# Four f32 matmuls whose results nobody reads, in TensorE's waits from the last piece of W_up to chunk 2 of W_down

## Chip, cores, metric

One core of one Trainium2 chip. The metric is the device time of one execution in microseconds (us); the profile's span, from its first to its last instruction, is some 1.3 us shorter. "The granted clock" is the share of its full speed at which TensorE is let run; the profile records it; "warm" and "cold" stand for 1.00 and 0.50. A "landing" is the arrival of a transfer's data. In the profile PE is TensorE, PEld its weight load, DVE VectorE, ACT ScalarE and SPq the queue that issues transfers; PSUM is the memory that TensorE writes.

## The reference, cut to what matters

A decode step: layer norm, attention over the last 4096 positions of a cache (4 sequences, 16 kv heads, 32 query heads), output projection and residual, then layer norm and a gated MLP with residual. The change touches the MLP.

```python
x = A_x                                                        # [4, 1, 576], bf16
h = x + _A_ref(_layernorm(x), A_k_cache, A_v_cache, A_wq, A_wo)
# _B_ref(layernorm(h), W_gate, W_up, W_down):
gate = jnp.einsum("bsd,df->bsf", x, W_gate)                    # F = 4608
up   = jnp.einsum("bsd,df->bsf", x, W_up)
hh   = gate * (gate > 0) * up
out  = h + jnp.einsum("bsf,fd->bsd", hh, W_down)
```

## The kernel before

All large inputs come through one DMA queue in one fixed order: wq, the K and V tiles, wo, W_gate, W_up, W_down. A transfer is only held back until the reader of the room it overwrites is done (in before the issue of W_down stood still 7.3 us for TensorE's line 34). W_down comes as chunks 0, 1 and 2 (1296 KB each) and chunk 3, split into rows 0-2, 3-5, 6-7 and 8 so that little work is left behind the last landing. The end of the kernel:

```python
for g in range(2):                       # 0: gate, 1: up
    for c in (4, 0, 1, 2, 3):            # c == 3 of up is a landing of its own
        part_ = c if c == 4 or (c == 3 and g) else 0
        for m in range(3):
            for j in range(4):
                deps = [("L", "gu", g, part_)] if first else []
                ...                      # 12 matmuls, 384 columns, 4 column groups side by side
# ... ReLU on ACT, product on DVE ("HH") ...
for r in range(9):                       # hh transposed by TensorE
    pe(("HTR", r), lambda e, r=r, dst=dst: e.transpose(...), [("HH", m) ...])
# ... copies to SBUF; two f32 and two bf16 matmuls start the sum with h ...
for j in range(4):                       # chunks of W_down
    for r in range(9):
        for n in range(2):               # 2 matmuls of 288 columns, side by side
            deps = []
            if n == 0:
                if r == 0 or (j == 3 and r in (3, 6, 8)):
                    deps.append(("L", "wd", j, r))       # waits for the landing
                ...
            pe(("DOWN", n), lambda e, ...: e.matmul(bank[n][...], ...), deps)
dve("OUT0", ...)                         # copy out, then the output DMA
```

`pe(name, fn, deps)` appends an instruction to TensorE's stream. TensorE's matmuls run in this order, and one that waits holds up those behind it (dose5 below shows the order: chunk 2 starts at 374.19 us, behind its fillers; late_idle shows the waiting: its 53 matmuls behind the one that names a wait name none, and all start after it, from 374.49 us).

## Time and profile before

| | before |
|---|---|
| time, median of the first three runs | 377.86 us (377.85 to 378.06) |
| span of the profiled execution | 376.6 us |
| TensorE busy | 208.8 us (55%) |
| DMA | 159.59 MB, 98.8% of the span, 424 GB/s |
| landing of rows 6 and 7 of chunk 3 (374.00 us) to last matmul's end | 0.74 us |
| end of the wait for row 8, the last piece (374.39 us), to last matmul's end | 0.35 us |

The page of before has the DMA queues with the share of the 16 engines' span that their packets took, and under its fourth heading the chain that ended last:

```profile
q1 hardware_dynamic: 6776, 159.59, 98.8%
...
DMA 56%; PE 21%; DVE 20%; issue 1%; SPq 1%; ACT 0%
```

The queue is busy nearly all the time. That points to a kernel bound by bytes; skip_chunk1 tests it below. Next the end of its chain of waits, in order of time (start, length, what):

```profile
341.69 32.31 DMA sb_arena<-in_B_W_down_dram
374.00 0.04 issue
374.04 0.70 PE psb L705 x6
374.74 0.43 DVE sb_out_sb L708
```

One copy closes the kernel. The timeline of before, TensorE only (start, length, engine, line, operation; in brackets how long the engine idled before it, and what ended that):

```profile
361.94 0.35 PE L667 MATMUL psb<-sb_arena,sb_hnT 128*32 128x384 bf16 x4 [0.71 <-DMA sb_arena<-in_B_W_up_dram]
...
363.95 0.27 PE L682 MATMUL psb<-sb_ident_b,sb_pp 128*128 128x128 bf16 x1 [1.34 <-DVE sb_pp L676]
...
368.13 1.16 PE L705 MATMUL psb<-sb_arena,sb_pp 128*32 128x288 bf16 x16 [1.37 <-DMA sb_arena<-in_B_W_down_dram]
...
371.23 1.03 PE L705 MATMUL psb<-sb_arena,sb_pp 128*32 128x288 bf16 x14 [1.82 <-DMA sb_arena<-in_B_W_down_dram]
...
373.33 0.55 PE L705 MATMUL psb<-sb_arena,sb_pp 128*32 128x288 bf16 x6 [0.46 <-DMA sb_arena<-in_B_W_down_dram]
374.04 0.66 PE L705 MATMUL psb<-sb_arena,sb_pp 128*32 128x288 bf16 x6 [0.17 <-DMA sb_arena<-in_B_W_down_dram]
...
374.39 0.10 PEld L705 LDWEIGHTS psb<-sb_arena,sb_pp 128*32 128x32 bf16 x2 [0.24 <-DMA sb_arena<-in_B_W_down_dram]
```

The brackets are TensorE's gaps, all but one here ended by a landing. The table of windows of before gives for each stretch the busy time and instruction count of each engine, then the granted clock, the DMA share and GB/s:

```profile
core 0: us, PE busy (x) PEld busy (x) DVE busy (x) ACT busy (x) POOL busy (x), PEclk, DMA share, GB/s
355.00:358.40 3.40, 3.40 (x44) 0.63 (x16) 0.00 (x0) 0.00 (x0) 0.00 (x0) 0.50 0.92 393
...
361.30:363.90 2.60, 0.67 (x12) 0.10 (x4) 1.49 (x3) 0.00 (x0) 0.00 (x0) 1.00 1.00 421
...
369.50:371.20 1.70, 0.00 (x0) 0.00 (x0) 0.00 (x0) 0.00 (x0) 0.00 (x0) 1.00 0.94 385
```

The clock was 0.50 in the first half of the MLP but 1.00 in all windows after 361.3 us, also in the gaps.

### The profile page before, as it was taken

The numbers are of one execution on the slowest core, as the hardware profiler recorded it, in microseconds if no ns is written. First come the engines' busy times: TensorE is split into PE (matmuls) and PEld (weight loads), VectorE is DVE, ScalarE is ACT, GpSimd is POOL, SyncE is SP. The second block draws the span as 40 slices with busy tenths as digits, with TensorE's granted clock in tenths as the row PEclk, the third lists the DMA queues.
The fourth block names the chain that finished last, engine by engine and source line by source line (L and its number), as shares of the span: only waits on it lengthen the run. The fifth ranks groups of instructions, "written<-read, shape, count | busy, mean of one in ns | idle before, by whom it ended". The sixth has DMA issues, their size and how long they took to land.

```text
span 376.6 us, 2562 instructions
## 1 busy us (share of the span) xinstructions
PE 208.8 (55%) x1456; PEld 37.6 (10%) x703; DVE 226.2 (60%) x164; ACT 54.3 (14%) x85; POOL 10.5 (3%) x29
## 2 busy tenths in 40 slices
PE   0304443249919191749282845664655687886674
PEld 0000000001101010001010100100000001002422
DVE  3078888779292959584847777665659423333220
ACT  3193000301000114010101140101010401112010
POOL 8200000000000000000000000000000000000000
PEclk9955888859968797687788796989696968998699
DMA  8999999999999999999999999999999999999996
GB/s 335 446 439 428 416 442 439 428 418 442 437 425 421 439 440 421 421 442 442 425 419 439 442 428 418 438 439 428 425 435 439 423 425 439 422 431 425 437 413 260
DMA packets 6802, 159.74 MB, mean 424 GB/s; under 512 B 764, under 2 KB 904, under 8 KB 1672
## 3 DMA queue, kind: packets, MB, share of 16 engines
q1 hardware_dynamic: 6776, 159.59, 98.8%
q8 instruction: 8, 0.13, 0.1%
q10 hardware_dynamic: 16, 0.01, 0.0%
q14 instruction: 2, 0.02, 0.0%
HBM read 159.58 MB, written 0.00 MB: 424 GB/s over the span
## 4 chain that ended last, share of the span: by engine, by line
DMA 56%; PE 21%; DVE 20%; issue 1%; SPq 1%; ACT 0%
DMA sb_arena<-in_A_k_cache_dram 48%; DVE sb_arena L425 16%; PE psb L34 13%; DMA sb_arena<-in_B_W_down_dram 9%; PE psb L449 4%; PE psb L510 3%; DVE sb_o_tmp L523 1%; DVE sb_pp L488 1%; PE psb L476 1%; SPq L284 0%; DVE sb_pp L471 0%; DVE sb_hx L454 0%; ACT sb_pp L468 0%; PE psb L705 0%; DVE sb_out_sb L708 0%
## 5 line engine op out<-in xcount | busy, mean ns | idle before, releaser
L425 DVE STREAM_TRANSPOSE sb_arena<-sb_arena 128x8192 f32<-128x8192 f32 (+1 forms) x19 | 139.9, 7365 | 66.4 <-DMA sb_arena<-in_A_k_cache_dram 66.4
L449 PE MATMUL psb<-sb_arena 128*32 128x512 bf16 x256 | 44.5, 640 | 118.8 <-DVE sb_arena L425 118.8
L34 PE MATMUL psb<-sb_arena,sb_pp 128*128 128x512 bf16 x382 | 107.3, 389 | 2.9 <-issue 2.8
L510 PE MATMUL psb<-sb_arena,sb_pp 128*128 128x512 bf16 x115 | 44.8, 389 | 8.9 <-DVE sb_o_tmp L523 8.9
L34 PE MATMUL psb<-sb_arena 128*32 128x512 bf16 x256 | 45.4, 645 | 0.0
L520 ACT COPY sb_o_tmp<-psb 32x512 f32<-32x512 f32 x32 | 18.5, 577 | 181.7 <-PE psb L34 181.4
L523 DVE TENSOR_TENSOR sb_o_tmp<-psb,sb_fm 32x512 f32<-32x512 f32 x32 | 21.7, 678 | 18.6 <-PE psb L34 18.1
L449 PEld LDWEIGHTS psb<-sb_arena 128*32 128x32 bf16 x256 | 9.7, 117 | 162.0 <-DVE sb_arena L425 131.8
L510 PEld LDWEIGHTS psb<-sb_arena,sb_pp 128*128 128x128 bf16 x128 | 12.8, 100 | 115.7 <-issue 115.7
L527 DVE TENSOR_REDUCE sb_o_sel<-sb_o_tmp 128x128 f32<-128x512 f32 x16 | 17.7, 1107 | 0.5
L468 ACT ACTIVATE sb_pp<-psb,sb_hx 128x1024 bf16<-128x1024 f32 x4 | 4.5, 1113 | 79.4 <-DVE sb_hx L465 79.4
L488 DVE TENSOR_TENSOR sb_pp<-psb,sb_m 128x1024 bf16<-128x1024 f32 x8 | 9.3, 1206 | 4.6 <-PE psb L476 4.6
L483 ACT ACTIVATE sb_pp<-psb,sb_m 128x512 bf16<-128x512 f32 x16 | 9.8, 698 | 14.6 <-PE psb L476 14.6
L526 DVE TENSOR_TENSOR sb_o_tmp<-sb_o_tmp,sb_fm 64x512 f32<-64x512 f32 x16 | 11.0, 689 | 0.5
L416 ACT COPY sb_arena<-sb_q_keep 32x256 bf16<-32x256 bf16 x8 | 9.7, 1448 | 0.1
L402 DVE CAST sb_pp<-psb 128x512 bf16<-128x512 f32 x1 | 2.4, 2425 | 10.1 <-PE psb L382 10.1
L471 DVE STREAM_TRANSPOSE sb_pp<-sb_pp 128x1024 bf16<-128x1024 bf16 x4 | 5.0, 1245 | 5.1 <-ACT sb_pp L468 5.1
L476 PE MATMUL psb<-sb_pp,sb_to_v 128*32 128x256 bf16 x64 | 4.3, 400 | 6.2 <-DVE sb_pp L471 6.2
L705 PE MATMUL psb<-sb_arena,sb_pp 128*32 128x288 bf16 x72 | 5.4, 288 | 3.8 <-DMA sb_arena<-in_B_W_down_dram 3.8
L708 DVE CAST sb_out_sb<-psb 32x288 bf16<-32x288 f32 x1 | 0.4, 446 | 9.7 <-PE psb L705 9.7
L454 DVE TENSOR_REDUCE sb_hx<-psb 128x1 f32<-128x1024 f32 x4 | 4.9, 1225 | 2.3 <-PE psb L34 2.3
L34 PE MATMUL psb<-sb_arena,sb_hnT 128*32 128x384 bf16 x80 | 6.3, 394 | 0.0
(123 smaller groups left out, 80.4 us busy)
## 6 DMA issues: line engine op xcount, KB each, us to landing
sb_arena<-in_A_k_cache_dram SPq DMA_DIRECT2D x16, 4096.0 KB, 26.1
sb_arena<-in_A_v_cache_dram SPq DMA_DIRECT2D x16, 4096.0 KB, 28.6
sb_arena<-in_A_wo_dram SPq DMA_DIRECT2D x1, 4608.0 KB, 25.3
sb_arena<-in_B_W_gate_dram SPq DMA_DIRECT2D x1, 4608.0 KB, 26.9
sb_arena<-in_A_wq_dram SPq DMA_DIRECT2D x1, 4096.0 KB, 13.1
sb_arena<-in_B_W_down_dram SPq DMA_DIRECT2D x3, 1296.0 KB, 30.9
sb_arena<-in_B_W_up_dram SPq DMA_DIRECT2D x1, 3456.0 KB, 27.8
sb_arena<-in_B_W_up_dram SPq DMA_DIRECT2D x1, 1152.0 KB, 30.3
```

Of the source, the lines that this page charges most:

```text
L34: return e.add_instruction(mybir.InstMatmult(name=e.bass.get_next_instruction_name(), engine=mybir.EngineType.PE, ins=[e.lower_ap(rhs), e. ...
L416: act("QW", lambda e, i=i, q=q: e.copy(out=bass.AP(tensor=arena, offset=32 * i * AW + 2 * i + q, ap=[[AW, 32], [512, 16], [136, 4], [32, 4]]),
L425: dve(("TRA", g), lambda e: e.transpose(out=dst, in_=src), [("L", "K", g)] if lo == 0 else [])
L449: fn = lambda e, out_=out_, lhsT=lhsT, rhs=rhs, start=start, stop=stop: e.matmul(out_, lhsT=lhsT, rhs=rhs, start=start, stop=stop, skip_gr ...
L476: pe(("RM", b, n // 2), lambda e, n=n, i=i: e.matmul(bank[6 if n < 2 else 0][32 * i:32 * i + 32, n % 2 * 256:n % 2 * 256 + 256], lhsT=to_v ...
L483: act(("EV", b, 0), lambda e, a=a: e.activation(out=bass.AP(tensor=pp, offset=2 * a, ap=[[PPW, 128], [8, 2], [32, 128], [1, 2]]), in_=bank ...
L488: dve(("EV", b, 1), lambda e, n=n: e.tensor_tensor(out=bass.AP(tensor=pp, offset=16 + 8 * n, ap=[[PPW, 128], [32, 128], [2, 4], [1, 2]]), ...
L510: fn = lambda e, lhsT=lhsT, rhs=rhs, k=k, j=j: e.matmul(bank[2 + j], lhsT=lhsT, rhs=rhs, start=(k == 0), stop=(k == 7), skip_group_check=True)
L520: act(("OSC", g), lambda e, j=j: e.copy(out=o_tmp[32 * j:32 * j + 32, 0:512], in_=bank[2 + j][32 * j:32 * j + 32, :]), [("PV", g), ("OSEL" ...
L523: dve(("OSD", g), lambda e, j=j: e.tensor_tensor(out=ot(32 * j, 32), in0=bank[2 + j][32 * j:32 * j + 32, :].rearrange("p (t d) -> p t d", ...
L526: dve(("OS", g), lambda e: e.tensor_tensor(out=ot(64, 64), in0=ot(64, 64), in1=fmb(64, 64), op=ALU.mult), [("OSC", g)])
L527: dve(("OSEL", g), lambda e: e.tensor_reduce(out=o_sel[:, qd, b, :], in_=o_tmp[:, 0:512].rearrange("p (t d) -> p d t", d=DH), axis=AX.X, o ...
```

## The change

The intent is to keep TensorE's activity up in its gaps, so that the granted clock doesn't fall before work that is waited for. Each filler multiplies constants and old values into a PSUM bank, and what it writes there is overwritten before anybody reads the bank, or never read: 256 columns before the last W_up piece, 384 before the transposes, 256 before chunk 1 and 512 before chunk 2 of W_down.

```diff
+        def keep_busy(n):
+            pe(None, lambda e: e.matmul(bank[7][:, 0:n], lhsT=toq[:, :, :, :].rearrange("p j t h -> p (j t h)"),
+                                        rhs=o_sel[:, 0, :, :].rearrange("p b d -> p (b d)")[:, 0:n], start=True, stop=True))
+
@@ after the 12 matmuls of one (g, c)
+                if g and c in (2, 3):
+                    keep_busy(128 * c)
@@ before the matmuls of chunk j of W_down
         for j in range(4):
             wv = arena[:, wd_off[j]:wd_off[j] + WDJ].rearrange("p (r n) -> p r n", n=D)
+            if j in (1, 2):
+                keep_busy(256 * j)
```

## The prediction

> What bounds the kernel now. The DMA stream. The page gives 159.59 MB on the one busy queue, whose packets fill 98.8% of the 16 engines' span of 376.6 us. At the end the chain of waits runs through the W_down transfer from 341.69 to 374.00 us, then 0.70 us of matmuls (line 705) and 0.43 us of the closing copy (line 708). All six W_down transfers are issued in one run from 339.89 us, when the last PV step has ended (timeline), so nothing that TensorE does later decides when a weight lands.
>
> TensorE waits; it is not waited for. In the timeline it idles 0.71 us before the last W_up piece, 1.34 us before the transposes (for the DVE products of line 676), and 1.37, 1.82, 0.46 and 0.17 us before the W_down pieces. The first chunk's matmuls end at 366.75 us and the next chunk is ready at 368.13 us, so a delay of up to 1.37 us before it is absorbed.
>
> What the change is after. It fills gaps so that the granted clock doesn't drop. [...] The trace agrees that it can halve (0.50 in the windows from 352 to 358.4 us[...]), but from 361.3 us to the end it is already 1.00 in every stretch, and the longest gap is 1.82 us. There is no slow clock left to mend. Even at half speed the last six matmuls' 0.70 us could grow by no more than about that; in the profiled run nothing can be won.
>
> What it adds. Four f32 matmuls, 128x128 weights, 256, 384, 256 and 512 columns, before the last W_up piece, the transposes, and chunks 1 and 2 of W_down. Each makes two records, as line 690's do: there four records of 288 columns, two column groups side by side, took 0.61 us until the next group began, so a record streams in about 0.25 us, 0.87 ns a column. My estimate is 1.74 ns a column for a whole f32 matmul: 0.45, 0.67, 0.45 and 0.89 us. Two f32 weight loads each (line 626: ten records in 2.25 us, mostly loads) may add up to 0.45 us where not hidden. Against the gaps of 0.71, 1.34, 1.37 and 1.82 us three fit surely; the first may push the last W_up piece back by 0.2 us at most, which the 1.37 us before chunk 1 absorbs. The fillers read SBUF constants, write a PSUM bank that nothing reads later, and move no DMA byte. None stands before the last pieces, where a delay would count.
>
> On the critical path: 0 us added, 0 us removed.
>
> Predicted time 377.9 us, range 377.4 to 378.4 (the three runs before spread 0.2 us; some room for another session). Chances: faster by over 2% 0.005, within 2% 0.985, slower by over 2% 0.01.
>
> What would show it. TensorE busy up by 2 to 4 us, all in 361 to 371.5 us. The gaps before the last W_up piece, the transposes and chunks 1 and 2 shrink by about the lengths above. Chunk 1 still starts near 368.1, chunk 2 near 371.2, the last pieces near 374.0 us; line 705's mean stays 288 ns; clock stays 1.00; from the last landing to the end stays about 2.6 us.
>
> What would make it wrong. A filler much slower than estimated (over 1.8 us) that delays chunk 2 and with it chunk 3; TensorE reads disturbing the DMA writes; or a clock that falls in unprofiled runs of before, so that the fillers save a few tenths of a us.

Two passages are cut from it where marked: claims about what makes the clock fall. The forecast's sum is the 377.9 us of before (377.86 us), with 0 us added and 0 us removed.

## The result, and the profile after

Ratios are the mean time of one kernel's fast runs over that of the other's of the same rounds, so not quite the ratio of the quoted medians.

| | before | after |
|---|---|---|
| time, median of 6 runs | 377.87 us (377.78 to 378.06) | 377.93 us (377.79 to 378.06) |
| ratio, 95% interval | | 1.0 (0.9988 to 1.0013) |
| TensorE busy | 208.8 us | 211.2 us |
| DMA | 98.8% of the span | 98.8% of the span |
| landing of rows 6 and 7 to end of span | 2.6 us | 2.6 us |

The end of the chain of waits of after:

```profile
341.83 32.36 DMA sb_arena<-in_B_W_down_dram
374.19 0.04 issue
374.24 0.70 PE psb L713 x6
374.94 0.43 DVE sb_out_sb L716
```

Line by line it is the chain of before, 0.2 us later. 0.14 us of that was there at 341.83, before the first filler. The same six matmuls take the same 0.70 us. The timeline of after with the four fillers (L552), TensorE only:

```profile
361.34 0.70 PE L552 MATMUL psb<-sb_o_sel,sb_toq 128*128 128x256 f32 x2
...
362.70 0.91 PE L552 MATMUL psb<-sb_o_sel,sb_toq 128*128 128x384 f32 x2
...
366.86 0.70 PE L552 MATMUL psb<-sb_o_sel,sb_toq 128*128 128x256 f32 x2
368.30 1.16 PE L713 MATMUL psb<-sb_arena,sb_pp 128*32 128x288 bf16 x16 [0.74 <-DMA sb_arena<-in_B_W_down_dram]
...
369.51 1.12 PE L552 MATMUL psb<-sb_o_sel,sb_toq 128*128 128x512 f32 x2
371.41 0.79 PE L713 MATMUL psb<-sb_arena,sb_pp 128*32 128x288 bf16 x10 [0.78 <-DMA sb_arena<-in_B_W_down_dram]
```

They took 0.70, 0.91, 0.70 and 1.12 us. The gaps before chunks 1 and 2 shrank from 1.37 and 1.82 to 0.74 and 0.78 us and still end with a landing. The table of windows of after, in stretches that answer to those shown of before:

```profile
355.00:358.40 3.40, 3.29 (x44) 0.68 (x16) 0.00 (x0) 0.00 (x0) 0.00 (x0) 0.50 0.91 388
...
361.30:363.90 2.60, 2.25 (x20) 0.70 (x8) 1.33 (x3) 0.00 (x0) 0.00 (x0) 1.00 1.00 417
...
369.50:371.20 1.70, 1.14 (x4) 0.30 (x2) 0.00 (x0) 0.00 (x0) 0.00 (x0) 1.00 0.97 399
```

The busy time rose where the fillers stand. The clock was 1.00 already and stayed there; the DMA share shows no loss.

So these two executions say "idle time filled, nothing else". Three readings remain.

- Theory: the DMA stream decides; the fillers lie in slack and there is no slow clock behind them.
- Rival A: in other executions of before the clock does fall in the tail, and the fillers mend that.
- Rival B: a gain is paid back by delays or by disturbed DMA writes.

### The profile page after: what moved, and what is told of

Its sections match the earlier page's. It is cut to its first block, busy times and chain, and to the rows that moved or that the text cites. A ratio compares the mean times of both kernels' runs of the same rounds, so it can differ in the third digit from the quotient of the medians.

```text
span 376.8 us, 2578 instructions
## 1 busy us (share of the span) xinstructions
PE 211.2 (56%) x1464; PEld 38.6 (10%) x711; DVE 226.5 (60%) x164; ACT 54.3 (14%) x85; POOL 10.5 (3%) x29
## 3 DMA queue, kind: packets, MB, share of 16 engines
q1 hardware_dynamic: 6776, 159.59, 98.8%
## 4 chain that ended last, share of the span: by engine, by line
DMA 56%; PE 21%; DVE 20%; issue 1%; SPq 1%; ACT 0%
DMA sb_arena<-in_A_k_cache_dram 48%; DVE sb_arena L425 16%; PE psb L34 13%; DMA sb_arena<-in_B_W_down_dram 9%; PE psb L449 4%; PE psb L510 3%; DVE sb_o_tmp L523 1%; DVE sb_pp L488 1%; PE psb L476 1%; SPq L284 0%; DVE sb_pp L471 0%; DVE sb_hx L454 0%; ACT sb_pp L468 0%; PE psb L713 0%; DVE sb_out_sb L716 0%
## 5 line engine op out<-in xcount | busy, mean ns | idle before, releaser
L449 PE MATMUL psb<-sb_arena 128*32 128x512 bf16 x256 | 42.5, 632 | 119.8 <-DVE sb_arena L425 119.8
L34 PE MATMUL psb<-sb_arena 128*32 128x512 bf16 x256 | 43.7, 643 | 0.0
L382 PE MATMUL psb<-sb_arena,sb_xnT 128*32 128x512 bf16 x16 | 2.5, 628 | 6.5 <-DMA sb_arena<-in_A_wq_dram 6.5
```

What stands on the lines that cost most here:

```text
L34: return e.add_instruction(mybir.InstMatmult(name=e.bass.get_next_instruction_name(), engine=mybir.EngineType.PE, ins=[e.lower_ap(rhs), e. ...
L449: fn = lambda e, out_=out_, lhsT=lhsT, rhs=rhs, start=start, stop=stop: e.matmul(out_, lhsT=lhsT, rhs=rhs, start=start, stop=stop, skip_gr ...
```

## The experiments

Twelve runs in three batches, each batch on one chip with its own runs of before. The comparison with the reference passed all twelve, even the three that leave out work of W_down; passing doesn't mean that they compute the right thing.

### First batch (before: 378.07 us median of 9, 377.88 to 378.26)

**after_again**: the change unedited, with more rounds.

> The changed kernel once more, with more rounds. Theory (the DMA stream decides, the fillers lie in idle time): the same as before within 0.15 us. Rival A (the fillers warm a clock that falls in some executions of before): faster by 0.1 to 0.3 us on the mean, and before shows some runs longer by as much. Rival B (a gain from the clock is paid back by delays or by disturbed DMA writes): the same total, but the last W_down piece lands later, or the last six matmuls are shorter than the 0.70 us of before.

Measured: 378.04 us (377.93 to 378.13, 5 runs), ratio 0.9999 (0.9986 to 1.0013). The last six matmuls again took 0.70 us, from 374.17 us. A tie a second time. On the mean neither rival shows.

**skip_chunk1**: before without one transfer of W_down; a wrong result.

```diff
-            wd_off.append(off)
+            wd_off.append(off if j != 1 else wd_off[0])
+            if j == 1:
+                continue
...
-                        if r == 0 or (j == 3 and r in (3, 6, 8)):
+                        if (r == 0 and j != 1) or (j == 3 and r in (3, 6, 8)):
```

> The kernel before, without the 1296 KB transfer of W_down chunk 1 (its matmuls read chunk 0's weights: wrong result on purpose). TensorE's work is unchanged. Theory: shorter by 1.327 MB at the page's 424 GB/s, 3.1 us, so about 374.8 us. If TensorE's tail decided, it would be the same or shorter by under 1 us.

Measured: 375.05 us, median of 4 (374.83, 374.94, 375.17 and 376.61). With TensorE's work unchanged, the median fell by 3.0 us, what the bytes said (3.1). Bytes bound the kernel. The 376.61 stands out; no profile caught it, and it comes back below the table of all executions.

**dose5**: the change with five fillers before chunk 2.

```diff
             if j in (1, 2):
-                keep_busy(256 * j)
+                for _ in range(1 if j == 1 else 5):
+                    keep_busy(256 * j)
```

> The changed kernel with five fillers of 512 columns before chunk 2 in place of one. Theory: each streams for 0.85 to 0.92 us, so chunk 2 starts at 373.9 to 374.2 us in place of 371.4, chunks 2 and 3 then run without a wait, and the last matmul ends 1.4 to 1.7 us later: 379.3 to 379.6 us. The slack there is gone and only what is over it shows. If TensorE time cost nothing at all: 377.9; if every microsecond of filler counted: +3.4 us or more.

Measured: 379.59 us (379.45 to 379.64), ratio 1.0039 (1.0027 to 1.0052), +1.5 us. The chain of waits of dose5:

```profile
368.43 1.28 PE psb L714 x18
369.70 4.49 PE psb L552 x10
374.19 2.36 PE psb L714 x36
```

Fillers now stand on the chain, and what exceeds the slack shows. The slack at this place is real and finite: four more fillers add 3.4 us of work (4.49 against 1.12) and 1.5 us of time.

**last_gap**: before with one filler, in front of the very last piece.

```diff
             for r in range(9):
+                if j == 3 and r == 8:
+                    keep_busy(512)
                 for n in range(2):
```

> The kernel before with one filler of 512 columns only, directly before the matmuls of the very last W_down piece (0.144 MB). Theory: no slack is there, so about all of its streaming time shows: 0.8 to 1.0 us longer, 378.7 to 378.9 us. If a filler's place didn't matter: 377.9 us.

Measured: 379.11 us, median (378.99 to 379.61), ratio 1.0029 (1.0017 to 1.0042), +1.04 us. A little above the range expected: the chain has 1.06 us for the filler. The same instruction costs nothing that shows before chunk 2 (after, ratio 1.0) and all of its time here.

This profile held a surprise. It has no filler before 374 us, so up to there it is the kernel before. Its table of windows, in stretches set where the clock changed:

```profile
361.01:364.43 3.42, 0.99 (x17) 0.43 (x10) 1.49 (x3) 0.00 (x0) 0.00 (x0) 1.00 1.03 430
364.43:367.84 3.41, 3.41 (x26) 1.59 (x25) 0.65 (x2) 0.58 (x1) 0.00 (x0) 0.50 1.00 426
367.84:371.25 3.41, 1.74 (x28) 1.02 (x22) 0.00 (x0) 0.00 (x0) 0.00 (x0) 1.00 0.96 400
```

The clock fell at 364.4 us, where the profile of before had 1.00, and chunk 0 ran slowly. Chunk 1's landing still was the later event (its first weight load still waited 0.2 us for it), so the time shows nothing. after_again's clock rose at 357.2 us, so its stretches lie nearly alike (0.4 us earlier), but it has the fillers:

```profile
360.66:364.07 3.41, 2.40 (x25) 0.73 (x9) 1.49 (x3) 0.00 (x0) 0.00 (x0) 1.00 1.02 423
364.07:367.49 3.42, 3.40 (x35) 1.94 (x35) 0.56 (x2) 0.58 (x1) 0.00 (x0) 1.00 0.98 415
```

With 2.40 us busy in the stretch in place of 0.99 the clock stayed up. The pair is not of one phase, but after_again's stretch begins at 360.66 us, between that of last_gap (361.01) and that of cold_tail (360.26, below), which has no fillers here and fell too; dose5, with the fillers, begins in between as well (360.47, 2.51 us busy) and stayed up. So rival A is half right: the clock of before does fall here in some executions, and the fillers do prevent it.

### Second batch (before: 378.03 us median of 11, 377.84 to 379.06)

**cold_tail** and **warm_tail**: what is a warm clock worth to the last six matmuls? Both multiply only chunk 0 and the last three rows of chunk 3 (wrong); TensorE should be idle for 7 us in the first, and is busy with fillers in the second.

```diff
# cold_tail
+                    if j in (1, 2) or (j == 3 and r < 6):
+                        if deps:
+                            pe(None, None, deps)       # wait for the landing only
+                        continue
# warm_tail: this as well
+            for _ in range((0, 3, 3, 2)[j]):
+                keep_busy(512)
             for r in range(9):
```

> The kernel before, but of W_down only chunk 0 and the last three rows of chunk 3 are multiplied (wrong result on purpose; every landing is still waited for), so TensorE is idle for 7.2 us before the last six matmuls. Theory: the granted clock falls to 0.50 in that stretch, the last six matmuls take 0.9 to 1.05 us in place of 0.70, and the whole is 0.15 to 0.35 us longer than before. That is the most that a filler could ever save at the end of this kernel.

> As cold_tail, with eight fillers of 512 columns in the 7.2 us of idle time (3, 3 and 2, before the waits for chunks 1, 2 and 3). Theory: the clock stays at 1.00, the last six matmuls take 0.70 us again, time as before (377.9 us), 0.15 to 0.35 us under cold_tail. If reads of TensorE disturbed the DMA writes, the last piece would land later here than in cold_tail, by more than the 0.2 us that runs differ by.

The chain of cold_tail:

```profile
374.16 0.14 issue
374.30 0.93 PE psb L713 x6
```

The chain of warm_tail:

```profile
374.14 0.14 issue
374.27 0.61 PE psb L715 x6
```

With the clock at 0.50 (cold_tail) and 1.00 (warm_tail) from 369 us on, the six matmuls take 0.93 and 0.61 us, so 0.32 us is what the clock can do there. (In both they start 0.14 us after the landing of rows 6 and 7, in before 0.04 us after it, so 0.61 isn't to be set against its 0.70.) The idle time didn't bring this clock down: in the profiled execution it had fallen at 363.7 us, chunk 0 was late, and it stayed at 0.50 through 5.3 us of idle time. All this speaks against rival B: there is hardly a gain to be paid back, and rows 6 and 7 landed at 374.14 us under 7 us of fillers against 374.16 us without. In time, cold_tail measured 378.29 us (378.17 to 378.37), 0.26 us over the median of before. Its ratio, 0.9999, hides this, because before had four long executions in this batch (378.49, 378.91, 378.95, 379.06).

warm_tail missed its expectation: 377.77, 378.01, 378.03, then 378.89, 380.39 and 380.44 us. Its profile is of a usual execution. An estimate for the long ones: warm_tail has no fillers before chunk 0, so its clock can fall at 363.7 to 364.4 us, as in cold_tail and last_gap; chunk 0 then ends 1.5 to 2.2 us late, and eight fillers, 6.9 us when warm, start late and slow. They end past 374 us by roughly 1 us (clock back at 367.8 us, last_gap's phase) to 2.5 us (back at 370.5 us, cold_tail's). The measured excess was 0.9 and 2.4 us. No profile caught one, so this stays an estimate.

**late_idle** and **late_filled**: the same question with the right result and more work at stake. All 54 matmuls of chunks 1 to 3 wait for the last landing, without and with eight fillers in the idle time.

```diff
# late_idle
-                        if r == 0 or (j == 3 and r in (3, 6, 8)):
-                            deps.append(("L", "wd", j, r))
+                        if j == r == 0:
+                            deps.append(("L", "wd", 0, 0))
+                        if j == 1 and r == 0:
+                            deps += [("L", "wd", 1, 0), ("L", "wd", 2, 0)] + [("L", "wd", 3, k) for k in (0, 3, 6, 8)]
# late_filled: this as well
+            if j == 1:
+                for _ in range(8):
+                    keep_busy(512)
```

> The kernel before, but all 54 matmuls of chunks 1 to 3 wait for the last landing (right result). Theory: 7.2 us idle drop the clock to 0.50, and the 54 matmuls run at half the clock for some 3.4 us or all the way: 4.5 to 6.3 us longer than before (27 pairs at 0.24 us cold, 0.1225 us warm).

> As late_idle, with eight fillers of 512 columns in the idle 7.2 us. Theory: clock 1.00, 27 pairs at 0.1225 us: 3.0 to 3.3 us longer than before, that is 1.3 to 3 us under late_idle. So the fillers do their work where the gap is long enough and the matmuls behind it are on the critical path. If the fillers have no effect on the clock, it equals late_idle.

The chain of late_idle, then that of late_filled:

```profile
374.35 0.14 issue
374.49 6.14 PE psb L711 x54
```

```profile
374.38 0.14 issue
374.52 3.52 PE psb L714 x54
```

late_idle: 383.14 us (382.6 to 383.75), +5.1. late_filled: 381.21 us (381.13 to 382.23), +3.2. Both as expected, with one long execution of late_filled. The device works: where a long wait is followed by work on the chain, fillers saved 1.9 us. In late_idle the clock fell at 369.6 us, in the idle time, and was back at 379.9 us, 5.4 us into the matmuls; in late_filled it was 1.00 from 366.2 to 378.0 us. (The 3.4 us of the expectation is the length of a cold stretch that TensorE filled, as in before from 344.80 to 348.21 us.) An estimate from these chains: a pair of matmuls costs about 0.24 us cold and 0.124 us warm.

### When does the clock fall?

The profiles allow a reading; the numbers here are of all fourteen, before and after included. In each the clock changes lie 3.41 us or a multiple apart, at a phase that differs between executions. In cold_tail the stretch before the fall, and the two after it, were:

```profile
360.26:363.68 3.42, 1.35 (x32) 0.10 (x4) 1.13 (x3) 0.00 (x0) 0.00 (x0) 1.00 1.00 419
363.68:367.09 3.41, 3.00 (x19) 1.49 (x21) 1.00 (x3) 0.58 (x1) 0.00 (x0) 0.50 1.01 423
367.09:370.50 3.41, 1.90 (x16) 0.90 (x12) 0.00 (x0) 0.00 (x0) 0.00 (x0) 0.50 1.00 423
```

With the profiles of before and after cut like this from 20 us to the end, 127 warm stretches, each of the 32 with at most 1.40 us of TensorE busy was followed by a cold one, and of the four with 1.43 to 1.51 us, two were. With all fourteen cut from about 340 us on, 101 warm stretches, each of the 11 with at most 1.40 us was followed by a cold one, and so were half_up's 1.48 us and half_down's 1.52 us. Those with 1.53 us or more were followed by a warm one, with two exceptions. One is a stretch in every profile around 347 to 353 us: 1.9 to 2.6 us busy, most of it f32 matmuls of 4 columns (2.25 of 2.45 us in before), and a fall after it in all. The other is the last one of after_third (1.71 us). So a fall goes with little busy time in the profile, but the busy time alone doesn't tell it.

For the way back no such figure comes out. After 340 us, cold stretches with up to 3.00 us busy (cold_tail) stayed cold and those with 3.21 us (half_down) or more recovered. But earlier in the kernel, in the attention, the clock came back after less, as in before:

```profile
245.81:249.23 3.42, 1.70 (x16) 0.38 (x12) 3.31 (x5) 0.00 (x0) 0.00 (x0) 0.50 1.05 450
249.23:252.64 3.41, 3.25 (x25) 0.33 (x6) 1.88 (x3) 0.00 (x0) 0.00 (x0) 1.00 0.89 384
```

The 1.70 us lie at the end of that stretch, from 247.53 us on. What brings the clock back stays open. For the fall, no long gap was needed: cold_tail's first stretch was busy for 1.35 of 3.42 us (40%), its longest gap was 1.14 us, and the one that runs on past its end 1.34 us.

From the busy times before a fall follows an estimate for before. A stretch that holds little but chunk 1 (1.28 us) should be followed by a cold clock from about 370 to 371.4 us, and the 18 pairs of chunks 2 and 3 then need about 4.3 us in place of the 2.2 us at full speed. The end comes 1.0 to 1.2 us later, or 0.5 us if the clock is back in time. Mostly before is spared: in those phases the clock has already fallen at 364 us, so that chunk 0 is late and lies in the same stretch. I put what is left at one execution in eight; the four long ones of the second batch were known when I did.

### Third batch (before: 377.96 us median of 9, 377.79 to 378.13)

**half_up** keeps only the first two fillers, **half_down** only the last two. If the estimate holds, half_up is worse than before, as its fillers remove the early fall that spares chunk 2.

```diff
# half_up
-            if j in (1, 2):
-                keep_busy(256 * j)
# half_down
-                if g and c in (2, 3):
-                    keep_busy(128 * c)
```

> The change with its first two fillers only (before the last W_up piece and before the transposes; none at W_down). Estimate worked out from the ten traces so far: the clock is looked at in fixed stretches of 3.41 us whose phase differs between executions; a warm stretch with under about 1.5 us of TensorE busy is followed by a cold one. Chunk 1 alone (1.28 us) in a stretch is too little, so the clock falls at 370 to 371.4 us and chunks 2 and 3 run cold. Before is mostly spared, because in those phases its clock has fallen once already at about 364 us and its late chunk 0 fills the stretch. The two fillers take that away. So: 30 to 45% of the executions longer by 0.5 to 1.2 us, the others as before. Rival (fillers in idle time never matter): all executions as before within 0.2 us.

> The change with its last two fillers only (before chunks 1 and 2 of W_down). Estimate as for half_up: no execution is longer than the others by more than 0.3 us, all near 377.9 to 378.2; the clock may be at 0.50 from 364 to 368 us in a quarter of the executions, which costs nothing as chunk 1 is waited for anyway.

half_up: 377.85, 377.90, 378.04, 378.53 and 378.95 us. Two of five are 0.5 and 0.9 us above its median, as the estimate said in number and size; ratio 1.001 (0.9996 to 1.0023). half_down: 377.86 to 378.00 us, ratio 0.9999 (0.9987 to 1.0012), none long. Two executions were longer with work added only in time that is idle in the profile, against the rival's expectation. But five runs of each are few: if 4 in 40 are long anyway (table below), two or more in five come by chance in about 8 of 100 cases. And half_up's profile was of a usual execution, clock 1.00 from 358.1 us on. The cause is supported, not seen.

**after_third** and **before_copy**: both kernels unedited.

> The whole change once more. Estimate: no execution more than 0.3 us above the others (none of 11 was so far); clock 1.00 from 360 us to the last matmul. Rival (the executions of before at 378.9 to 379.1 us come from the DMA or the chip, not from the clock): they turn up here as often as in before, of which 3 in 26 were so long.

> The kernel before, unchanged, for another profile and more executions. Estimate: about one execution in eight some 0.9 to 1.2 us longer (clock fallen at about 370 us, chunks 2 and 3 cold), the rest within 0.3 us. If the profile falls on a usual one, its clock stays 1.00 after 368 us.

after_third: 377.88 us (377.78 to 378.02), ratio 0.9999 (0.9986 to 1.0011). before_copy: 377.95 us (377.88 to 378.06), ratio 1.0001 (0.9988 to 1.0013), no long execution; in its profile the clock stayed 1.00 from 359.5 us past the last matmul.

All executions together:

| kernel | executions | over 0.4 us above its batch's median of before |
|---|---|---|
| before (and before_copy) | 6 + 9 + 11 + 9 + 5 = 40 | 4 (378.49, 378.91, 378.95, 379.06), all in the second batch |
| half_up | 5 | 2 |
| half_down | 5 | 0 |
| after | 6 + 5 + 5 = 16 | 0 |

The long ones of before have the size that the estimate gives, and 4 in 40 is near one in eight. But the estimate was made after them; the third batch, which could have tested it, had none in 14 executions of before (at one in eight, chance gives that in about 15 of 100 cases). And they all fell on one chip, after wasn't run on that chip, and 0 in 16 would happen by chance in about one of five cases if the true rate were 4 in 40 (0.9 to the 16th power is 0.19). That the fillers remove them is likely and not shown.

No execution that is called long here was profiled, so that they come from the DMA or the chip isn't ruled out. The record gives each execution's mean granted clock. It was lowest in the long ones of half_up (0.796 and 0.800 against 0.810 to 0.837), in the two longest of warm_tail (0.797 against 0.814 to 0.823) and in skip_chunk1's 376.61 us (0.786 against 0.807 to 0.817), which fits the clock. But in the second batch the four long ones of before had 0.796 to 0.814 and the seven others 0.796 to 0.819, so this settles nothing. last_gap's 379.61 us and late_filled's 382.23 us, 0.5 and 1.0 us over their medians, are as unexplained.

## Why the prediction was right, and where it wasn't

- **The time.** Predicted 377.9 us, measured 377.93 us. What bounds the kernel was right: skip_chunk1 took away 1.327 MB and 3.0 us, with TensorE's work unchanged.
- **Sizes.** The four ranges (0.45 to 0.9, 0.67 to 1.1, 0.45 to 0.9, 0.89 to 1.34 us) held 0.70, 0.91, 0.70 and 1.12 us. The table of windows has 3.4 us more TensorE busy between 348 us and the end (20.91 against 17.55), within the 2 to 4 us.
- **Slack.** No landing was missed. dose5 (+1.5 us) and last_gap (+1.04 us) show that the slack has an end, and that the last pieces have none. The prediction counts six transfers of W_down issued from 339.89 us; there are seven, and chunk 0's was issued at 332.1 us. As the last was issued at 346.8 us, before any filler, its conclusion stands. Its "last landing" at 374.00 us is that of rows 6 and 7.
- **Starts.** Chunks 1 and 2 and the last pieces started 0.17, 0.18 and 0.20 us later than before; most of it (0.14 us) was there before any filler. Line 705's mean held (a median of 286 ns in both).
- **The step that failed.** "There is no slow clock left to mend" was read from one execution. last_gap and cold_tail, the same kernel up to that point, fell to 0.50 at about 364 us. The longest-gap argument behind it (no gap over 1.82 us) failed too: a stretch of cold_tail with no gap above 1.34 us lost its clock. How long a gap must be for a fall was not shown by any trace. The trace of before could have warned: a clause cut from the prediction laid its fall at 351.6 us to idle time, but TensorE was busy for 2.45 us of the stretch before it, with no gap over 0.81 us. That this error did not move the median is luck: the early fall hides behind chunk 1's landing.
- **The named risk.** The prediction listed "a clock that falls in unprofiled runs of before" as worth a few tenths of a us. The fall is real. Where it should hurt it would cost up to about 1.2 us in few executions, on the mean about 0.1 us (4 long ones in 40, by 0.5 to 1.0 us). That is under what the intervals (about 0.13%, 0.5 us) can tell.
- **Disturbed DMA writes** didn't show: warm_tail and cold_tail had rows 6 and 7 landed at 374.14 and 374.16 us.

## What to carry to other kernels

Before you fill a gap, ask what the work behind it waits for; if a landing comes later anyway, a warm clock wins nothing (last_gap's cold stretch from 364.43 us lay before chunk 1's landing and cost nothing that shows), and in the place without slack the filler costs its whole time (last_gap, +1.04 us). The phase of the clock's stretches differs between executions (boundaries at 360.26 us in cold_tail, 361.01 in last_gap, 361.86 in before), so one profile can't show that the clock is safe: look at several, and at the spread of the times. And filling the early gaps alone may be worse than filling none: half_up had two long executions in five, half_down, with the late fillers alone, had none, and so few runs can be chance.
